# A gated mix of two attentions on one core: 776 instead of 756 score tiles on VectorE, in a new hand-laid order

## The chip, the cores and the metric

The kernel runs on one core of a Trainium2 chip. The metric is the device time of one execution in microseconds (us), the median of several runs. The engines of the core work side by side, each through its own list of instructions in order: TensorE (PE in the profile; PEld is its weight load), VectorE (DVE), ScalarE (ACT), GpSimd (POOL) and SyncE (SP, which only issues transfers here). They wait for one another through semaphores.

## The reference

The input x (2048 rows of 512, bf16) goes through two attentions with 32 heads of 16 each, and a gate mixes them. Part A is a linear attention with learnt softmax features, part B is ordinary softmax attention.

```
qkv = (x @ wqkv)                       # 32 heads of 16, for A and for B with weights of their own
# A
phi_q = [softmax(q @ w_phi), softmax(-q @ w_phi)];  phi_k likewise
o = phi_q @ (phi_k^T v) / (phi_q @ sum(phi_k) + 1e-6);   a = o @ A_wo
# B
p = softmax(q k^T / 4);   o = p v;     b = o @ B_wo
g = sigmoid(sum(x * gate_w))
out = g * a + (1 - g) * b
```

## The kernel before

Part B is nearly all of the work. It is cut into 32 blocks: a block is four heads and 512 queries. For each head of a block, the 2048 keys make 16 tiles of 128 keys by 512 queries, so a block has 64 score tiles and the kernel 2048. A score tile is one product (`qk_mm`, L994) that uses a strip of 32 rows of TensorE's array; the four heads of a block lie on four different strips, so up to four score products can run at once. Its result fills one bank of PSUM. There are six banks for scores (`bS`), one more for other work (`bM`) and one that gathers the weighted sums of a block (`bO`, `psO`).

A tile's exponential is made in one of two ways:

- On ScalarE: one instruction for two tiles in neighbouring banks (`add_exp`, L1115). The result goes to `Ebuf`, and one weighted sum for each tile (`pv_mm`, L1136) adds it to `psO`. Four such sums with 32 columns of the array each run at once.
- On VectorE: a conversion to int16 whose bits, read as bf16, are a rough exponential (`add_group`, L1084). Tiles go in groups of up to four. GpSimd adds a constant to all of a group's words in place of a second and a third conversion (`shifted`, L1060), and TensorE adds up all three versions in three weighted sums a tile (`add_pvd`, terms t, s and m). Two conversions of one group can be joined to one instruction over two banks (`Plan.join`, L1074); the table's `pairs` say which.

`DN` holds how many of each block's 64 tiles go to VectorE; its sum is 756. The groups of tiles use buffers in turn, from two rings (`PHASES`) that change at block 16 and at block 27.

Beside this run the projections of q, k and v for both parts, part A as a whole, the division by the sums of each block (a chain of small transfers through DRAM) and the output projection. Projections (`columns`, L754) use the array in strips of 32 columns, as the weighted sums do.

The order of each engine's instructions isn't found by the program when it is built: it is written out in `TABLE`, made beforehand by a planner that isn't in the file. Each number is the place of an operation in the list `P.ops`; an entry below zero stands for a filler, an operation that adds zeros or whose result nobody reads. `homes` gives the bank of each result. `Plan.place` reads the table, and `Plan.emit` writes the instructions with the waits that follow from data and banks. A wait is put in front of an instruction, and what stands behind it on its engine waits too.

At the start, `warm_fn` (L705) issues six products of ones while x is on its way.

Of the kernel before, what the change touches and what calls it, by code (L numbers as in the profile page):

```python
# [30 lines left out]
DN = (16, 24, 18, 24, 26, 26, 26, 20, 22, 22, 24, 18, 26, 24, 20, 26, 30, 22, 24, 26, 22, 24, 30, 26, 18, 22, 36, 18, 24, 24, 32, 16)  # L31
# [3 lines left out]
SIZES = (2, 2)  # L35
STICK = 58.273
# [59 lines left out]
    ),  # L96
    "act": (
# [32 lines left out]
    ),  # L130
# [465 lines left out]
def _build(ctx, nc, A_x, A_wqkv, A_w_phi, A_wo, B_wqkv, B_wo, gate_w, out):  # L596
# [105 lines left out]
    def warm_fn(e):  # L702
        ins = None
        for _ in range(6):
            ins = e.matmul(psM, lhsT=ones[:, 0:128], rhs=ones, start=True, stop=True)  # L705
        return ins
# [956 lines left out]
```

## Time and profile before

| | |
|---|---|
| median of 3 runs | 660.67 us |
| lowest and highest | 659.57 and 660.74 us |
| profiled execution, first to last instruction (span) | 657.6 us; the page has no other time of it |
| granted TensorE clock | 1.000 |
| PE busy | 649.1 us, 99% of the span |
| ACT busy | 635.1 us, 97% |
| DVE busy | 609.4 us, 93% |
| POOL busy | 410.8 us, 62% |

A busy engine in this table is one with at least one instruction under way; instructions overlap, matmuls above all, so the share doesn't say how densely they follow one another. For that the starts of instructions are read from the timeline. The chain of work that ended last is followed back from the last instruction, at each step to what released it or to the instruction before it on its engine. "x4" in a row of the timeline stands for four merged instructions.

### The profile page before, as it was taken

The page shows a single profiled execution, that of the slowest core. Times are in us where ns is not written, and L with a number is a line of the kernel's source. Part 1 is how long each engine was busy: PE and PEld are TensorE (multiplying, and loading weights), DVE is VectorE, ACT ScalarE, POOL GpSimd, SP SyncE. Part 2 cuts the span into 40 slices and gives each one's busy share as a digit, 9 for nine tenths or more (in the row PEclk, how much of TensorE's full clock was granted, in tenths as well). Part 3 has the DMA queues.
Part 4 walks back from the last instruction along what each step waited for, and adds up shares of the span by engine and source line. Part 5 has one row for each costly group of instructions (what it writes and reads, how often), then busy time and mean ns, then how long its engine had stood idle before and what let it go on. Part 6 is the DMA issues. An engine that isn't in the chain of part 4 may idle for free.

```text
span 657.6 us, 20651 instructions
## 1 busy us (share of the span) xinstructions
PE 649.1 (99%) x8820; PEld 227.3 (35%) x8820; DVE 609.4 (93%) x963; ACT 635.1 (97%) x720; POOL 410.8 (62%) x437
## 2 busy tenths in 40 slices
PE   8999999999999999999999999999999999999997
PEld 4333333434333333333233233322333333332333
DVE  6999899999998789999999999999999989999985
ACT  6999999999999999999999999999989999999996
POOL 7575367465665446486467876575867566656853
PEclk9999999999999999999999999999999999999999
DMA  6530101001010000000012431233211633134132
GB/s 131 104 100 12 33 12 27 11 11 19 11 27 10 16 18 8 19 17 14 23 37 47 100 77 33 63 78 68 48 51 35 102 56 83 35 63 103 44 84 48
DMA packets 67947, 30.94 MB, mean 47 GB/s; under 512 B 53208, under 2 KB 62808, under 8 KB 67856
## 3 DMA queue, kind: packets, MB, share of 16 engines
q1 hardware_dynamic: 65840, 28.82, 19.6%
q8 instruction: 69, 1.13, 0.7%
q10 hardware_dynamic: 1632, 0.79, 0.5%
q14 instruction: 22, 0.18, 0.1%
q0 software_dynamic: 384, 0.02, 0.1%
HBM read 7.87 MB, written 8.88 MB: 25 GB/s over the span
## 4 chain that ended last, share of the span: by engine, by line
PE 85%; DVE 12%; ACT 1%; issue 1%; DMA 1%; SPq 0%; DVEq 0%
PE psO L1136 32%; PE psS L994 30%; PE psS L754 15%; DVE Tx_t L1084 3%; PE psS L1417 3%; DVE Ty_t L1084 1%; DVE oT_t L1084 1%; DVE Wp_t L1084 1%; PE psS L842 1%; ACT E_t L1115 1%; DVE Tz_t L1084 1%; PE psS L1514 1%; PE psS L855 1%; PE psO L1126 1%; DMA phiK_t<-in_A_x_dram 1%
## 5 line engine op out<-in xcount | busy, mean ns | idle before, releaser
L1115 ACT ACTIVATE E_t<-psS 128x1024 bf16<-128x1024 f32 x643 | 601.9, 1068 | 11.2 <-PE psS L994 10.3
L994 PE MATMUL psS<-qz_t,kTB_t 32*128 32x512 bf16 (+1 forms) x2054 | 267.5, 383 | 2.8 <-ACT E_t L1104 0.6
L1084 DVE TENSOR_SCALAR Tx_t<-psS 128x512 int16<-128x512 f32 x246 | 163.2, 682 | 10.5 <-PE psS L994 9.4
L994 PEld LDWEIGHTS psS<-qz_t,kTB_t 32*128 32x128 bf16 x2054 | 71.8, 91 | 226.4 <-ACT E_t L1115 102.9
L1136 PE MATMUL psO<-E_t,vaug_t 128*32 128x512 bf16 x1292 | 119.0, 384 | 0.0
L1060 POOL INT64_ADD vA_t<-vA_t x72 | 71.6, 999 | 19.0 <-PE psO L1136 13.7
L1084 DVE TENSOR_SCALAR Ty_t<-psS 128x512 int16<-128x512 f32 x114 | 76.5, 682 | 4.8 <-PE psS L994 4.5
L1060 POOL INT64_ADD Ty_t<-Ty_t x42 | 44.0, 1048 | 18.5 <-PE psO L1136 18.1
L1060 POOL INT64_ADD Ty_t<-Tx_t x29 | 30.1, 1038 | 39.0 <-DVE Tx_t L1084 32.7
L1136 PE MATMUL psO<-vA_t,vaug_t 128*32 128x512 bf16 (+1 forms) x520 | 52.6, 384 | 0.0
L1136 PE MATMUL psO<-Ty_t,vaug_t 128*32 128x512 bf16 x440 | 45.4, 384 | 0.0
L1136 PEld LDWEIGHTS psO<-E_t,vaug_t 128*32 128x32 bf16 x1292 | 30.2, 95 | 39.5 <-issue 28.4
L1084 DVE TENSOR_SCALAR oT_t<-psS 128x512 int16<-128x512 f32 x62 | 41.7, 682 | 1.5 <-PE psS L994 1.0
L1084 DVE TENSOR_SCALAR Tz_t<-psS 128x512 int16<-128x512 f32 x60 | 40.2, 680 | 2.1 <-PE psS L994 1.8
L1060 POOL INT64_ADD vA_t<-Tx_t x22 | 22.7, 1032 | 31.0 <-DVE Tx_t L1084 24.1
L1060 POOL INT64_ADD phiQT_t<-Tx_t x19 | 18.9, 993 | 29.1 <-DVE Tx_t L1084 28.0
L1084 DVE TENSOR_SCALAR vA_t<-psS 128x512 int16<-128x512 f32 x54 | 36.2, 682 | 0.7 <-PE psS L994 0.3
L1084 DVE TENSOR_SCALAR WAT_t<-psS 128x512 int16<-128x512 f32 x52 | 35.2, 682 | 1.4 <-PE psS L994 1.2
L754 PE MATMUL psS<-Wp_t,xT_t 128*32 128x512 bf16 x512 | 35.8, 382 | 0.0
L754 PE MATMUL psS<-xT_t,WB_t 128*32 128x512 bf16 x480 | 34.9, 382 | 0.2
L1084 DVE TENSOR_SCALAR Wp_t<-psS 128x512 int16<-128x512 f32 x50 | 33.8, 683 | 0.9 <-PE psS L994 0.7
L1060 POOL INT64_ADD WoB_t<-oT_t x19 | 19.3, 1016 | 20.7 <-DVE oT_t L1084 16.5
(165 smaller groups left out, 920.1 us busy)
## 6 DMA issues: line engine op xcount, KB each, us to landing
dpq<-EA_t SPq DMA_DIRECT2D x16, 256.0 KB, 2.3
Rb_t<-lr SPq DMA_DIRECT2D x120, 32.0 KB, 1.9
dpo<-kv_t SPq DMA_DIRECT2D x16, 128.0 KB, 1.8
qz_t<-qz_t SPq DMA_DIRECT2D x120, 16.0 KB, 1.8
Tf_t<-Tf_t SPq DMA_DIRECT2D x60, 32.0 KB, 2.0
WB_t<-in_B_wqkv_dram SPq DMA_DIRECT2D x3, 384.0 KB, 3.6
out_dram<-WvA_t SPq DMA_DIRECT2D x8, 128.0 KB, 2.0
out_dram<-WB_t SPq DMA_DIRECT2D x6, 128.0 KB, 2.0
```

The costliest lines, as they stand in the source:

```text
L754: ins = e.matmul(out[32 * i:32 * i + 32, :], lhsT=lhsT[:, 32 * i:32 * i + 32], rhs=rhs, start=start, stop=stop, tile_position=(0, 32 * i))
L842: mms = [lambda e, ap, i=i, t=t: e.matmul(ap[:, 128 * i:128 * (i + 1)], lhsT=xT[:, t, NQ * c + 128 * i:NQ * c + 128 * (i + 1)], rhs=W_B[:, ...
L855: mms = [lambda e, ap, i=i, t=t: e.matmul(ap[:, 256 * i:256 * (i + 1)], lhsT=xT[:, t, NQ * c + 128 * (2 * hf + i):NQ * c + 128 * (2 * hf + ...
L994: return e.matmul(bank, lhsT=kT_B[32 * i:32 * i + 32, ROW[b // 2] % 2, 128 * kt:128 * (kt + 1)], rhs=qz[32 * i:32 * i + 32, b // 2 % 4, b ...
L1060: op = P.add("pool", P64 + W64 * size, d_prio(g["ts"][0]) - 5.0 + (0.0 if key == "s" else M_LATE), lambda e: e.int64_add(words(dst), words ...
L1084: ops.append(drain(f, mm, "dve", 0.70, d_prio(d), lambda e, ap, q=q: e.tensor_scalar(quarter(tb, q).bitcast(I16), ap, EXPB, 0.0, op0=ALU.a ...
L1115: op = P.add("act", EXP_OVH + 0.4267 * n, 0.0, lambda e: e.activation(Ebuf[:, j // 2 % EPAIRS, 512 * SZ[0] * (j % 2):512 * SZ[0] * (j % 2) ...
L1126: ins = e.matmul((psO if bank is None else bank)[32 * i:32 * i + 32, :], lhsT=zero[:], rhs=xT[:, 0, 0:NQ], start=bank is not None, stop=ba ...
L1136: return e.matmul(psO[32 * i:32 * i + w, :], lhsT=vaug[:, kt, o:o + w], rhs=rhs, start=start, stop=stop, tile_position=(0, 32 * i), skip_g ...
L1417: mms = [lambda e, ap, n=n, f=f: e.matmul(ap[:, 64 * n:64 * n + 64].rearrange("p (s g j) -> p s g j", s=2, j=4), lhsT=ident[:], rhs=es[n][ ...
L1514: mms = [lambda e, ap, g=g: e.matmul(ap[:, 64 * g:64 * g + 64], lhsT=qT(g)[:, 128 * j:128 * (j + 1)], rhs=kzbd[:, g, 0:64], start=True, st ...
```

## The change

Twenty tiles move from ScalarE to VectorE: ten entries of `DN` rise by 2. `TABLE` is new throughout: the order on all five engines, the banks, and the pairs of conversions. By the words that came with the change, the new order was laid out with GpSimd's and VectorE's use of a shared port on a first-come basis and with TensorE's signals spread out in time. What can be counted in the two tables:

| entries | before | after |
|---|---|---|
| SP | 259 | 259 |
| ACT | 693 | 683 |
| PE | 3017 | 3014 |
| of these fillers (below zero) | 23 | 1 |
| DVE | 963 | 1013 |
| POOL | 433 | 441 |
| pairs of conversions | 59 | 29 |

The warming products go from six to eight, a new kind of filler (-4, one product of ones into a score bank, with no wait for data) stands once near the start, and the two rings of buffers go on, at a change of phase, where the phase before stopped, in place of starting at their first buffer.

```
-DN = (16, 24, 18, 24, 26, 26, 26, 20, 22, 22, 24, 18, 26, 24, 20, 26, 30, 22, 24, 26, 22, 24, 30, 26, 18, 22, 36, 18, 24, 24, 32, 16)
+DN = (16, 24, 18, 26, 26, 26, 28, 20, 22, 24, 24, 18, 28, 24, 20, 26, 32, 22, 26, 26, 22, 26, 30, 26, 20, 22, 36, 20, 24, 24, 34, 16)
+TURNS = (0, 0)
 TABLE = {
     "pe": (
-        33, 72, 74, 86, 76, 80, 78, 88, 801, 803, 83, 807, 802, 804, 808, 90, 92, 93, 94, 95, 914, 912, 871, 867, 97, 98, 99, 100, 811,
...
+        33, 72, 74, -4, 86, 76, 80, 78, 88, 801, 803, 83, 807, 802, 804, 808, 90, 92, 93, 865, 914, 912, 817, 94, 95, 97, 98, 99,
...
         op = Op("pe", 0.215, 0.0, None, "idle")
-        op.deps, op.kind = list(self.ground), "zero"
+        op.deps, op.kind = [] if kind == -4 else list(self.ground), "zero"
...
-            op.fn = self.idle if kind == -1 else self.idle_o
+            op.fn = {-1: self.idle, -2: self.idle_o, -4: self.early}[kind]
...
     def warm_fn(e):
         ins = None
-        for _ in range(6):
+        for _ in range(8):
             ins = e.matmul(psM, lhsT=ones[:, 0:128], rhs=ones, start=True, stop=True)
...
-    count = [0] * len(PHASES)
+    count, at = [0] * len(PHASES), [(0, 0)]
     for n, g in enumerate(groups):
...
+        if g["ph"] == len(at):
+            more = count[g["ph"] - 1] - TURNS[g["ph"] - 1]
+            at.append(tuple((a + more) % len(ring) for a, ring in zip(at[-1], PHASES[g["ph"] - 1][1:])))
         count[g["ph"]] += 1
-        g["t"], g["s"] = rt[k % len(rt)], rs[k % len(rs)]
+        g["t"], g["s"] = (ring[(k + a) % len(ring)] for a, ring in zip(at[g["ph"]], (rt, rs)))
...
+    P.early = lambda e: e.matmul(psS[:, 1536:2048], lhsT=ones[:, 0:128], rhs=ones, start=True, stop=True)
```

More of the change, by code (lines that the diff above doesn't have):

```diff
@@ L349 @@
     "homes": (
-        "6705645027467514305342074350243502534104260164320524035135602350263510365015430143620420342604261461024510346013546026140264052310"
-        "5230152035062546025460520625306235102241052450613506452062540264506250426450624045260452452064052065420624502645032650624065235602"
-        "4506420523602520452360542654062405624062405624602560245560425605426504256024606254062554026504620562452406524056204254605240520462"
-        "0642506452602540562054260546256032065426042650420563206245065420253065426043260235602460250423015601350263506230654205230562450624"
@@ L354 @@
-        "6025602506452064250463260244502640241012654062504562406520462563020546202640526045265406250264540265604256034260352405246052064526"
-        "0462506426054260524560423106420602456054205462405620542654065240526404256045260542604256062504265405264062540625046256042605246504"
-        "2605642052402456053260524054205246054256024625064256105362053642045246502405642602305626504260532605320542504260452605426054620456"
-        "2045206425650465204653206523506420542606542064362036520630523230654206425602540654206254602654062540523052643034625042564052604534"
@@ L358 @@
-        "2035013640163561430163015042506245062406452604256042506452605260526025405240652045624562045604250646254065204526045620563263560365"
-        "0240564250436524062405240562405624062365024056254056204562406420546254062305623053620362036042650426503625032560245602460542502465"
-        "0326054625062450635206426402245403601360234502456035461052145042654062504260545216450620452640526045625406240652640524064250325602"
-        "4650320654206530624302456042505246052460264056240526045264026540260542650426052460254602546052460256045256042052540526506230564206"
@@ L362 @@
-        "524054025043560"
+        "6705645027467051435041234560351603610350625460532506245062054625062506452506325062460524056250642650246502450652406246504250426502"
+        "5406524025604562046264052064524605260452405620530416445036205632502356024560526045240652640530164024032651032146020142601420614621"
+        "4062140621042654025402543024532351036154205345234152054306240362463025360235106340153103416340613562035620352503210524150230513402"
+        "5124052034520325046520426540261046210420154201540251402514204502146026140264162041620416214325303165063251032501325031650351603561"
@@ new lines @@
+        "3561035163513051024501356431253026053605236052460524603015402156012402504526506210461053610531603563105630160315036156360153026350"
+        "2630526350362056320526350624506235024506246043260532603426054320643206430264032453205624056245604205623056425406240235012514036250"
+        "3240632460135025362035206320654205452016210642016402346240562540265402605462506352046206230524503265042532504530623506235026405624"
+        "0523650635023601364016431040364023462064230642310513605130154125102315032053215012305236502305630156302464063221352063620532062450"
@@ new lines @@
+        "6324603402463013051420353025360456250321503201524105214051240520354203452043540345051345102350123154205102450123150425140254301531"
+        "4613046120461260421540214501240521046203420125305420513205425140215021504126502450325063015361035015301653061305163420634620452026"
+        "4026402635206320663521041265042640126061351605310531630416240126504235032463104530164016240216046215413465130522062465042560320463"
+        "0135023460235602435130402346203431052316536013560264310530610351604301643026305235023506234602536203520653605320563256042506426023"
@@ L363 @@
+        "6103106310520604246404013"
     ),
@@ L416, in __init__ @@
         self.writer, self.readers = {}, {}
-        self.idle, self.idle_o, self.misc, self.every, self.never, self.ground = None, None, [], [], None, []
+        self.idle, self.idle_o, self.misc, self.every, self.never, self.ground, self.early = None, None, [], [], None, [], None
     def add(self, eng, dur, prio, fn, reads=(), writes=(), after=(), name="", sem=None, lat=0.0):
```

512 rows, old and new, of the table TABLE are left out of this document.

## The prediction

> **What bounds the kernel now.** I read four views in this order: the busy times and the chain of the page, the stretches of 60 us, the timeline of TensorE, and the waits. First the page: share of the span, instructions, and by engine the chain of work that ended last.
>
> ```profile
> span 657.6 us, 20651 instructions
> ...
> PE 649.1 (99%) x8820; PEld 227.3 (35%) x8820; DVE 609.4 (93%) x963; ACT 635.1 (97%) x720; POOL 410.8 (62%) x437
> ...
> PE 85%; DVE 12%; ACT 1%; issue 1%; DMA 1%; SPq 0%; DVEq 0%
> ```
>
> Three engines are nearly full, and the chain runs 85% through TensorE (PE). "Busy" alone doesn't say that an engine works at its pace, so I look at the paces. The timeline gives starts and durations (us); I read starts against starts.
>
> ```profile
> 200.95 0.60 PE L994 MATMUL psS<-qz_t,kTB_t 32*128 32x512 bf16 x5
> ...
> 642.29 0.40 PE L1136 MATMUL psO<-E_t,vaug_t 128*32 128x512 bf16 x4
> 642.52 0.39 PE L1136 MATMUL psO<-vA_t,vaug_t 128*32 128x512 bf16 x4
> 642.84 0.39 PE L994 MATMUL psS<-qz_t,kTB_t 32*128 32x512 bf16 x3
> 643.16 0.40 PE L1136 MATMUL psO<-E_t,vaug_t 128*32 128x512 bf16 x4
> 643.38 0.39 PE L1136 MATMUL psO<-vA_t,vaug_t 128*32 128x512 bf16 x4
> ```
>
> Four weighted sums (L1136, one for each strip of 32 columns) start together and the next four start 0.22 us later (643.16 to 643.38): this is one PE step. From sums to score products (L994, strips of 32 rows) it takes 0.32 (642.52 to 642.84) and back again 0.32 (642.84 to 643.16). So each alternation between the two costs 0.10 above a step. Three score products on different strips take 0.39 in all, but the five at 200.95 take 0.60: a product whose strip is taken by an earlier one of the same run adds 0.21, one more step.
>
> The paces of the other two engines, from rows that merge several instructions of one kind, and from the chain:
>
> ```profile
> 203.74 2.87 ACT L1115 ACTIVATE E_t<-psS 128x1024 bf16<-128x1024 f32 x3
> 641.22 1.89 DVE L1084 TENSOR_SCALAR Ty_t<-psS 128x512 int16<-128x512 f32 x3
> 50.10 1.13 DVE Tz_t L1074
> ```
>
> With the mean durations of the groups below (1068 and 682 ns), an exponential of two tiles follows another after (2.87 - 1.07) / 2 = 0.90 us on ScalarE (ACT), and a conversion of one tile on VectorE (DVE) after (1.89 - 0.68) / 2 = 0.60. A paired conversion (two tiles, L1074) holds the chain for 1.13.
>
> ```profile
> L1115 ACT ACTIVATE E_t<-psS 128x1024 bf16<-128x1024 f32 x643 | 601.9, 1068 | 11.2 <-PE psS L994 10.3
> L1084 DVE TENSOR_SCALAR Tx_t<-psS 128x512 int16<-128x512 f32 x246 | 163.2, 682 | 10.5 <-PE psS L994 9.4
> L1060 POOL INT64_ADD vA_t<-vA_t x72 | 71.6, 999 | 19.0 <-PE psO L1136 13.7
> L1247 DVE TENSOR_TENSOR oT_t<-Tf_t,Rb_t 128x512 bf16<-128x512 f32 x15 | 10.7, 716 | 0.0
> ```
>
> Now the stretches (us busy and instructions of PE, weight loads, DVE, ACT, POOL; then granted clock, DMA share, GB/s):
>
> ```profile
> 60.00:120.00 60.00, 60.00 (x855) 20.95 (x843) 54.52 (x85) 60.00 (x72) 33.35 (x36) 1.00 0.11 21
> 180.00:240.00 60.00, 59.97 (x857) 20.57 (x854) 51.94 (x79) 59.94 (x72) 31.79 (x36) 1.00 0.08 18
> 300.00:360.00 60.00, 59.00 (x806) 19.88 (x798) 57.83 (x98) 59.19 (x68) 37.99 (x38) 1.00 0.11 27
> 360.00:420.00 60.00, 59.88 (x794) 19.81 (x790) 58.61 (x89) 60.00 (x69) 43.89 (x44) 1.00 0.32 73
> ```
>
> In 60:120, 180:240 and 360:420 ACT has no idle time to speak of: there it is a bound of its own beside PE. DVE is fullest in 360:420 (58.61 of 60) and has 8 us to spare in 180:240. At one place DVE alone carries the chain without a break; a few of its pieces:
>
> ```profile
> 306.14 1.20 DVE Tz_t L1084 x2
> 307.34 0.60 DVE Tx_t L1084
> 307.94 0.60 DVE vaug_t L862
> ```
>
> The waits, last (us in total, times, longest):
>
> ```profile
> PEld psS L994 <- ACT E_t L1115: 102.9, 258, 0.6
> PEld psO L1136 <- issue: 87.0, 360, 0.4
> ...
> ACT E_t L1115 <- PE psS L994: 10.3, 27, 0.8
> DVE Tx_t L1084 <- PE psS L994: 9.4, 25, 1.1
> ```
>
> The 102.9 look like a stall of PE behind ACT, but 102.9 / 258 is 0.40 each, and an alternation puts 0.32 between two starts whether anybody is waited for or not, so most of it is the alternation itself. PE works near its pace, ACT is just behind, and DVE is third.
>
> **The change part by part.** The counts of operations below are counted in DN and in the order tables, those of the kernel and those of the diff; none is a time.
>
> *Twenty tiles from ACT to DVE.* ACT does 646 exponentials before ((2048 - 756) / 2: 643 in the row above and three done in halves) and 636 after: 10 x 0.90 = 9.0 us less. This counts where ACT is a bound, the three full stretches, 180 of 657.6 us: -2.5. Where PE ends last it is worth nothing.
>
> *DVE.* The pairs in the table fall from 59 to 29, so single conversions go from 638 to 718: 80 x 0.60 - 30 x 1.13 = 48.0 - 33.9 = +14.1 us. DVE idles 657.6 - 609.4 = 48.2 us, which hides it on the whole; it isn't hidden where DVE carries the chain. The longest such place, around 300 us, is fed by blocks 13 to 15 (block 13 begins at exponential 270 of 646), and their DN isn't raised. I take +0.4, for the pairs that are split there. Bounds: 0, and 12% of the time at 14.1 / 609.4, that is +1.8. If the cover is gone, see the first rival.
>
> *PE, more sums.* The groups go from 198 to 202, each with three terms; the sums over exponentials go from 337 operations to 334, one step each. 12 - 3 = 9 steps more, at 0.22: +2.0 us.
>
> *PE, fillers.* 23 filler operations of four zero products leave (the table has 23 entries of -1, and none after). 23 x 0.22 = 5.1 us. The row of the source view and its busy tenths over 40 slices:
>
> ```profile
> L1126 PE MATMUL psO<-xT_t,zero_t x92: 379/379/390, 17.2 to 595.9; 128*32 128x512 bf16 x92
> ...
> busy tenths in 40 slices 0110000000010000000000223430002000012000
> ```
>
> Most stand in slices 23 to 27 (360 to 440 us), where ACT and DVE are full and PE would have waited; so the bounds are 0 and -5.1 and I take half, -2.5.
>
> *PE, order of the score products.* In the old order 107 score products find their strip of rows taken in their run, in the new one 81: 26 x 0.21 = -5.5. Runs of score products go from 595 to 600, and all changes between row-wise, column-wise and whole-array work from 1222 to 1227: +5 x 0.10 = +0.5. Bounds of the first: 0, where the second product waited for its bank anyhow, and -5.5. I take -5.5, by the x5 row, where nothing but the strip held it.
>
> PE together: +2.0 - 2.5 - 5.5 + 0.5 = -5.5 us, between +2.5 and -8.1. It counts where PE sets the end, outside the stretches given to ACT (27%) and DVE's 12%: 61% of it, -3.4.
>
> *The start.* Two more warming products, and one more (entry -4) behind the first two transposes of x. Here is the start, and the load that the chain waits for:
>
> ```profile
> 0.77 2.72 PE L705 MATMUL psS<-const-bfloat16-1.0 128*128 128x512 bf16 x6 [0.77 <-PEq L1648]
> 3.33 0.58 PE L1529 MATMUL psS<-ident_t,phiK_t 128*128 128x128 bf16 x4
> ...
> 5.91 0.40 PE L1529 MATMUL psS<-ident_t,phiK_t 128*128 128x128 bf16 x4 [0.35 <-DMA phiK_t<-in_A_x_dram]
> ...
> 1.65 4.21 DMA phiK_t<-in_A_x_dram
> ```
>
> The six take 2.72, about 0.43 apart, so two more push the first transpose from 3.33 to about 4.2 and the products behind it by as much, less what they waited for loads. The transposes at 5.91 wait for the load that ends at 5.86 whatever comes before, so I cost it at 0; without that cover it is +0.9, and a clock that comes up earlier could give back a few tenths (four 128-column products took 0.58 at 3.33 and 0.40 at 5.91).
>
> *POOL and SP.* Groups of four go from 180 to 186 and groups of two from 18 to 16. Each has two shifted adds; a whole one takes 1.0 us, so POOL gains 12 adds of 1.0 and loses 4 shorter ones: about +10 on 410.8. It stays off the path unless an add comes late for its sums; behind it on POOL are only further adds. SP issues 259 operations before and after, in another order; of the chain 1% is DMA, so I take 0. The ring of buffers now goes on where the phase before it stopped: no instruction changes.
>
> *First-come port use.* That POOL's adds and some DVE operations hold each other up shows in one row: the 15 products of L1247 average 716 ns against 682 of the conversions, 15 x 0.03 = 0.5 us, all off PE. So a layout that avoids it can bring at most about that, and I put down 0. The Trainium skill's page "SBUF — State Buffer" ("Who interferes with whom") says that a DVE instruction with two SBUF inputs and a GpSimd instruction that reads SBUF exclude each other, the loser waiting the whole instruction through. By that rule the 15 could wait up to 1.0 us each, an estimate of 15 us on DVE to be saved. The trace agrees on the direction and not on the size; were it so, the time would fall as in the third rival, whose chance holds it.
>
> **Sum:** -2.5 (ACT) - 3.4 (PE) + 0.4 (DVE) = -5.5, so a span of 652.1. The page gives no time of the profiled execution beside its span; the median of the runs shown, 660.67, is 3.07 above it. 652.1 + 3.1 = 655.2, and I say 655.
>
> **The rivals.**
>
> *DVE becomes the bound (slower).* It has one fixed order, and each conversion frees a bank that a score product waits for. In 360:420 it has 1.4 us of 60 left, and +14.1 over the kernel is 1.3 for each 60. It decides if DVE keeps the waits it has now: then it needs 609.4 + 14.1 + 48.2 = 671.7 of span, 674.8 in time; with half of the waits kept, 650.7. The break-even is at 34 us of the 48.2. For it: thirty pairings are given up at the same time as the load rises. Against it: 8 us are free in 180:240, and DVE's waits in the groups above are for PE, which the change relieves. I say 667, between 663 and 675.
>
> *Nothing comes of it.* The strips that were taken twice waited for banks anyhow, the fillers stood in waits, and ACT isn't on the chain (1%): PE is then +2.5, less what ACT's full stretches give, -2.5. Time 660.7, between 658 and 663. For it speaks that chain; against it that PE's waits for ACT are mostly alternations, so PE's steps do count.
>
> *More than the counts say.* PE's steps shrink by the whole 8.1 and the waits of ACT for PE (10.3 of the 11.2) go too, ACT then takes its 9.0 over the whole kernel: 657.6 - 9.0 = 648.6 of span, 651.7, and down to 645 if part of those 10.3 goes.
>
> *The clock falls without the fillers (slower).* The granted clock is 1.00 in all stretches quoted. If a gap grew long enough to lose it, steps would take about twice as long for a while, as at the start (0.58 against 0.40): six such losses of 3 us each, with the steps in them at half pace, cost about 9 us: 664 on top of the forecast, 670 on top of no gain. Against it: the longest wait of PE in the rows above is 0.6 us, and a filler adds only 0.22 to one. The Trainium skill's page "TensorE: Matmul & The Clock Gate" ("HAM oscillation") says that a PE left idle for more than about 3.4 us goes back to half its clock; no run here shows that, and no gap here is near it.
>
> **How the numbers follow.** As summed: 0.52, with its own range of 651 to 659. More: 0.14. Nothing: 0.17. DVE: 0.14. Clock: 0.03. The range that leaves out about 2 in 10 runs from 647 to 663. About 0.2% (1.3 us) is what a measurement of this kernel can tell from no change. Faster by more: 0.52 + 0.14 + 0.04 of "nothing" = 0.70; within: 0.10; slower: 0.03 + 0.14 + 0.03 = 0.20.
>
> **What would show it.** Right: about 633 exponentials in the row of L1115, the same pace of 0.90, no L1126 in the middle, ACT busy near 626, PE's share of the chain at 80% or more, and runs of score products with fewer long rows. Wrong: DVE's share of the chain at 25% or more, with long rows of waits of PE's weight loads for Tx_t and Ty_t; or a granted clock under 1.00; or ACT's idle time before L1115 (11.2) above 20, which would mean that the saved exponentials came back as waits.

## The result, and the profile after

The changed kernel takes 654.65 us (median of 4 runs, 654.29 to 655.40), the kernel before 660.12 us on the same chip (4 runs, 658.95 to 660.74). The ratio is 0.9913 with a 95% interval of 0.9889 to 0.9938: 5.5 us faster, against a forecast of 655.0. A second set of runs gave 0.9918 [0.9905, 0.9932]. The profiled execution took 655.01 us with a span of 653.1, so the time lies 1.9 us above the span.

The page after: span, busy time, share of the span and instructions of an engine, and by engine the chain of work that ended last.

```profile
span 653.1 us, 20595 instructions
...
PE 646.6 (99%) x8771; PEld 229.7 (35%) x8771; DVE 615.8 (94%) x1013; ACT 626.6 (96%) x710; POOL 420.4 (64%) x445
...
PE 85%; ACT 10%; DVE 4%; issue 0%; DVEq 0%
```

The loads moved as counted: ACT from 635.1 to 626.6 us busy, DVE from 609.4 to 615.8, POOL from 410.8 to 420.4. The chain changed its second engine. DVE had 12% of it and ACT 1%; now ACT has 10% and DVE 4%. DVE has more work and yet less of the chain, so this comes with the new order (the split pairs are part of it) and not from the load.

The groups after (busy, mean ns of one, idle time before and its releaser; L1131 are the exponentials, L1100 the conversions, L1076 POOL's adds):

```profile
L1131 ACT ACTIVATE E_t<-psS 128x1024 bf16<-128x1024 f32 x633 | 592.4, 1059 | 15.3 <-PE psS L1010 14.5
...
L1100 DVE TENSOR_SCALAR Tx_t<-psS 128x512 int16<-128x512 f32 x268 | 175.3, 680 | 3.5 <-PE psS L1010 2.7
...
L1076 POOL INT64_ADD vA_t<-vA_t x68 | 68.6, 1014 | 19.4 <-PE psO L1152 19.0
```

There are ten exponentials fewer (633 for 643). ACT's idle time before them rose from 11.2 to 15.3 us, so part of the saved work came back as waits. DVE's idle time before Tx_t fell from 10.5 to 3.5. Now the stretches of 60 us, in the columns used before:

```profile
60.00:120.00 60.00, 60.00 (x845) 21.79 (x846) 55.63 (x92) 59.29 (x71) 35.55 (x39) 1.00 0.09 21
...
180.00:240.00 60.00, 59.94 (x855) 21.34 (x851) 54.53 (x86) 59.27 (x70) 35.88 (x39) 1.00 0.09 18
...
300.00:360.00 60.00, 59.94 (x841) 20.86 (x842) 59.38 (x100) 59.26 (x68) 39.04 (x40) 1.00 0.16 45
360.00:420.00 60.00, 59.95 (x810) 20.64 (x802) 59.24 (x99) 59.50 (x71) 45.26 (x46) 1.00 0.31 76
```

In 60:120, 180:240 and 360:420 ACT was at 60.00, 59.94 and 60.00 busy; it now has a little air. DVE is fuller in all four, 59.4 of 60 around 300 us, where it carried the chain before. There the chain after reads (start, duration, engine, product):

```profile
304.20 0.55 PE psO L1152 x8
304.75 0.34 PE psS L1010 x4
305.08 0.54 PE psO L1152 x8
```

That is TensorE alternating between sums and scores at its own pace: 0.55 for eight sums is two steps and one change (0.22 + 0.32). DVE is fuller here and nobody on the chain waits for it.

I read the same gain from three ledgers, each made from all starts of one engine in the two traces: its work at pace (the time between two starts when nothing holds the second), and its idle time above pace.

| from first to last instruction of the kind | work at pace | waits above pace |
|---|---|---|
| PE, all products | 620.7 to 616.7 (-4.0) | 32.4 to 32.0 (-0.4) |
| ACT | 620.8 to 611.7 (-9.1) | 30.7 to 35.2 (+4.5) |
| DVE | 595.4 to 609.1 (+13.7) | 58.6 to 41.2 (-17.4) |

By this ledger PE turned its 4.0 us into time almost in full, ACT gave half of its 9.1 back as waits, and DVE took on 13.7 and lost 17.4 of waits. How PE's row splits depends on the paces: with one fixed pace for a step (0.21 to 0.22) and one for an alternation (0.32) the same starts give -2.9 and -1.5. Its sum, -4.4, doesn't depend on them; DVE's row is good to about 1 us.

By kinds of product on PE, each run of one kind timed to the start of the next: scores -3.5, sums +3.0, fillers -7.1, projections +4.4 (cut off by scores more often: 127 times for 103), products over the whole array -1.2.

Where these 4.4 us lie shows when both traces are cut at the same score products, counted by their starts:

| score products | before | after |
|---|---|---|
| 1000th to 1400th | 122.7 us, with 56 filler and 232 projection products | 122.2 us, with 0 and 304 |
| 1400th to 1800th | 124.5 us, with 8 and 368 | 119.7 us, with 0 and 272 |

The first stretch (323 to 446 us before) is the one in which most fillers stood. It takes the same time in both orders, but the new one has 72 projection products there in place of the fillers. The stretch behind it has 96 fewer (their time falls by 6.0 us), and is 4.8 us shorter. So the new order does useful work where the old one only filled. That moving these projections alone would bring the gain isn't shown: no run does that.

### The profile page after: what moved, and what is told of

Its sections match the earlier page's. It is cut to its first block, busy times and chain, and to the rows that moved or that the text cites. A ratio compares the mean times of both kernels' runs of the same rounds, so it can differ in the third digit from the quotient of the medians.

```text
span 653.1 us, 20595 instructions
## 1 busy us (share of the span) xinstructions
PE 646.6 (99%) x8771; PEld 229.7 (35%) x8771; DVE 615.8 (94%) x1013; ACT 626.6 (96%) x710; POOL 420.4 (64%) x445
## 4 chain that ended last, share of the span: by engine, by line
PE 85%; ACT 10%; DVE 4%; issue 0%; DVEq 0%
PE psO L1152 32%; PE psS L1010 30%; PE psS L767 15%; ACT E_t L1131 10%; PE psS L1433 2%; PE psS L868 1%; PE psS L855 1%; DVE Tx_t L1100 1%; PE psS L1530 1%; DVE Ty_t L1100 1%; PE psS L1517 1%; PE psS L718 1%; DVE vA_t L1100 1%; DVE Wp_t L1100 0%; PE psS L1392 0%; PE psS L1473 0%
## 5 line engine op out<-in xcount | busy, mean ns | idle before, releaser
L1131 ACT ACTIVATE E_t<-psS 128x1024 bf16<-128x1024 f32 x633 | 592.4, 1059 | 15.3 <-PE psS L1010 14.5
L1100 DVE TENSOR_SCALAR Tx_t<-psS 128x512 int16<-128x512 f32 x268 | 175.3, 680 | 3.5 <-PE psS L1010 2.7
L1010 PEld LDWEIGHTS psS<-qz_t,kTB_t 32*128 32x128 bf16 x2054 | 72.9, 91 | 224.2 <-ACT E_t L1131 112.5
L1152 PE MATMUL psO<-E_t,vaug_t 128*32 128x512 bf16 x1272 | 124.4, 385 | 0.0
L1100 DVE TENSOR_SCALAR Ty_t<-psS 128x512 int16<-128x512 f32 x122 | 81.2, 683 | 5.5 <-PE psS L1010 5.2
L1076 POOL INT64_ADD vA_t<-vA_t x68 | 68.6, 1014 | 19.4 <-PE psO L1152 19.0
L1152 PE MATMUL psO<-vA_t,vaug_t 128*32 128x512 bf16 x534 | 53.1, 385 | 0.0
L1100 DVE TENSOR_SCALAR Tz_t<-psS 128x512 int16<-128x512 f32 x74 | 49.0, 681 | 2.5 <-PE psS L1010 2.0
L1076 POOL INT64_ADD Ty_t<-Ty_t x43 | 43.3, 1008 | 10.1 <-PE psO L1152 9.0
L1152 PEld LDWEIGHTS psO<-E_t,vaug_t 128*32 128x32 bf16 x1272 | 32.4, 95 | 42.8 <-issue 33.5
L1100 DVE TENSOR_SCALAR oT_t<-psS 128x512 int16<-128x512 f32 x66 | 43.9, 682 | 3.2 <-PE psS L1010 2.4
L1152 PE MATMUL psO<-Ty_t,vaug_t 128*32 128x512 bf16 (+1 forms) x450 | 45.9, 385 | 0.0
L1100 DVE TENSOR_SCALAR vA_t<-psS 128x512 int16<-128x512 f32 x66 | 44.1, 681 | 0.9 <-PE psS L1010 0.7
L1100 DVE TENSOR_SCALAR WAT_t<-psS 128x512 int16<-128x512 f32 x66 | 43.8, 680 | 0.4 <-PE psS L1010 0.4
L767 PE MATMUL psS<-Wp_t,xT_t 128*32 128x512 bf16 x512 | 41.2, 382 | 0.0
L1100 DVE TENSOR_SCALAR Wp_t<-psS 128x512 int16<-128x512 f32 x56 | 37.5, 681 | 0.5 <-PE psS L1010 0.5
L1076 POOL INT64_ADD phiQT_t<-Tx_t x19 | 19.3, 1015 | 22.9 <-DVE Tx_t L1100 20.7
L1076 POOL INT64_ADD Ty_t<-Tx_t x24 | 23.6, 984 | 15.6 <-DVE Tx_t L1100 15.5
L1076 POOL INT64_ADD WoB_t<-oT_t x19 | 18.9, 993 | 20.5 <-DVE oT_t L1100 18.5
L1076 POOL INT64_ADD WoA_t<-Tz_t x19 | 19.7, 1039 | 15.7 <-DVE Tz_t L1100 7.8
```

The source lines that it names most:

```text
L767: ins = e.matmul(out[32 * i:32 * i + 32, :], lhsT=lhsT[:, 32 * i:32 * i + 32], rhs=rhs, start=start, stop=stop, tile_position=(0, 32 * i))
L1010: return e.matmul(bank, lhsT=kT_B[32 * i:32 * i + 32, ROW[b // 2] % 2, 128 * kt:128 * (kt + 1)], rhs=qz[32 * i:32 * i + 32, b // 2 % 4, b ...
L1076: op = P.add("pool", P64 + W64 * size, d_prio(g["ts"][0]) - 5.0 + (0.0 if key == "s" else M_LATE), lambda e: e.int64_add(words(dst), words ...
L1100: ops.append(drain(f, mm, "dve", 0.70, d_prio(d), lambda e, ap, q=q: e.tensor_scalar(quarter(tb, q).bitcast(I16), ap, EXPB, 0.0, op0=ALU.a ...
L1131: op = P.add("act", EXP_OVH + 0.4267 * n, 0.0, lambda e: e.activation(Ebuf[:, j // 2 % EPAIRS, 512 * SZ[0] * (j % 2):512 * SZ[0] * (j % 2) ...
L1152: return e.matmul(psO[32 * i:32 * i + w, :], lhsT=vaug[:, kt, o:o + w], rhs=rhs, start=start, stop=stop, tile_position=(0, 32 * i), skip_g ...
```

## The experiments

My theory was the sum of the prediction: fillers, taken strips and ACT's load each bring their part, and DVE's additions hide. The rivals: PE ends last everywhere, so that each step saved on PE counts in full and a relief of ACT brings nothing (A); the fillers keep the clock up (B); a taken strip stands in a wait, so that untangling it brings nothing (C); ACT is the bound (D); only the new order as a whole gains (E); DVE has become the bound (F). All ratios are against the kernel before on the same chip.

**One relief at a time, on the old order.** Three edits of the kernel before: without the 23 fillers; with 15 pairs of tiles swapped within their groups, so that 17 score products fewer find their strip taken; and with 21 exponentials over one tile in place of two, 21 x (1054 - 638 ns) = 8.7 us less for ACT by the means in its trace.

```
old_nofill:  + TABLE["pe"] = tuple(k for k in TABLE["pe"] if k != -1)
old_strips:  + SWAPS = ((856, 858), (865, 869), ...)     # 15 pairs of score products
             + for a, k in SWAPS: swap a with k in TABLE["pe"], a + 1 with k + 1 in TABLE["dve"]
old_half:    + HALF = tuple(range(12, 642, 30))
             + w = n - (j in HALF)                       # tiles that exponential j covers
```

> The old order without its 23 fillers (four zero products each), all else as before. Mine, from the sum of the prediction: they stood in waits for the most part, so half of 5.1 us at most: 0 to -2.5, I expect -1.5 us against the kernel before (ratio 0.998). Rival A (PE ends last everywhere, so each of its steps counts): the 7.1 us that the fillers and the gaps behind them take in the old trace come off whole, ratio 0.989 to 0.992. Rival B (the fillers keep the clock up): granted clock under 1.00 and a longer time.

> The old order with 15 swaps of two tiles within their group, so that 17 fewer score products find their strip of rows taken in their run; nothing else moves. Mine: each is worth one step on PE (322 ns for a run without, 534 with one), 17 x 0.21 = 3.6 us of PE's work; the part that reaches the end as in the prediction's sum, 0.61 of it: -2.2 us, ratio 0.9967. Rival A (PE ends last everywhere): -3.6, 0.9945. Rival C (a taken strip stands in a wait for a bank): 0, 1.000.

> The old order, with 21 of the 646 exponentials, spread over the kernel, done for their first tile only (the second tile's result is left out, its bank is freed with the first): ScalarE has 21 x 0.43 = 9.0 us less to do, as after the change, and nothing else differs. Mine: only where ACT is a bound beside PE, 27% of the span: -2.5 us, ratio 0.996. Rival D (ACT is the bound): -9, 0.986. Rival A (PE ends last everywhere): 0.

Measured: 1.0003 [0.9990, 1.0016] without fillers, 1.0002 [0.9988, 1.0015] with the swaps, 1.0001 [0.9991, 1.0011] with the lighter ACT. The bounds leave at most 0.7, 0.8 and 0.6 us of gain (0.10%, 0.12% and 0.09% of 660); by my sum's weights they were worth 1.5 (2.5 at 61%), 2.2 (17 x 0.21 = 3.6 at 61%) and 2.4 (8.7 at 27%). In the traces, the swaps took 0.5 us off the time of the score products on PE, not 3.6, so the rest must have come back as waits there. Without the fillers, the stretch from the 1000th to the 1400th score product still takes 122.2 us (122.7 with them). ACT's busy time fell by 5.3 us (635.1 to 629.8), and it waits longer: its exponentials waited 10.3 us in 27 waits before, and in old_half (total, times, longest):

```profile
ACT E_t L1117 <- PE psS L995: 14.5, 41, 0.9
```

My theory fell here. Rival C holds, within 0.8 us. Rival A is right for ACT alone: it asked for 7.1 us from the fillers and 3.6 from the swaps, and neither came. B's lower clock didn't show either (1.000 without fillers).

**All three together on the old order**, and the changed kernel itself beside it.

```
old_all:  the three edits above in one kernel
new_again: the changed kernel, unedited
```

> The three together on the old order: no fillers, 17 fewer taken strips, 21 exponentials for one tile only (the second tile's result is left out). Mine: PE and ACT are bounds in turn, so a relief of both brings more than the sum of the parts: -1.5 - 2.2 - 2.5 = -6.2 at least, -8 if so; ratio 0.988 to 0.991, that is the gain of the change or more without its new order. Rival E (the new order itself, its fewer waits, is what gains): -3 at most, 0.995 or above.

> The changed kernel itself again, beside the three that follow, so that they can be compared with it on one chip. Every theory: ratio to the kernel before 0.991 as measured.

Measured: 0.9991 [0.9979, 1.0002], 659.01 us; the changed kernel 0.9918 [0.9905, 0.9932], 654.56. So with fewer steps on PE and nearly the same relief for ACT, and without a microsecond more on DVE, the old order gains at most 1.4 us, as rival E has it. From old_all's page:

```profile
PE 646.7 (98%) x8728; PEld 227.1 (35%) x8728; DVE 608.3 (93%) x963; ACT 628.7 (96%) x720; POOL 411.0 (63%) x437
...
PE 81%; DVE 15%; ACT 1%; issue 1%; DMA 1%; POOL 0%; SPq 0%
```

PE is busy for as long as after the change (646.7 and 646.6) and the kernel isn't faster. PE's work at pace is 615.0, 5.7 less than before; its waits are 37.5, 5.1 more. DVE's share of the chain rose from 12% to 15%, and I asked next whether DVE holds it.

**The same with a lighter DVE.** 34 single conversions cover 64 of 512 columns.

```
old_light: old_all, and   w = 64 if q == 0 and g["n"] % 5 == 2 and g["n"] > 9 else NQ
```

> The old order relieved on all three engines: no fillers, 17 fewer taken strips and 21 exponentials for one tile only, as in old_all, and 34 single conversions narrowed from 512 to 64 columns (the rest of those tiles is left out), 34 x 0.47 = 16 us less on VectorE. old_all, without the last, gained 0.6 us although PE and ACT had 6 to 9 us less to do. Theory G (the three engines are bounds in turn, and in old_all DVE was the one left): 5 to 7 us faster than old_all, ratio 0.989 to 0.992. Theory H (what is left is the fixed order: each engine waits where the order makes it wait for the hand-over of another, whatever its load): under 2 us against old_all, 0.996 to 0.999.

Measured: 0.9977 [0.9965, 0.9989], 658.71 us (before: 659.55). Its page:

```profile
PE 646.5 (98%) x8728; PEld 226.4 (34%) x8728; DVE 595.7 (91%) x963; ACT 629.0 (96%) x720; POOL 410.7 (63%) x437
...
PE 84%; DVE 8%; ACT 6%; DMA 1%; issue 1%; POOL 0%; SPq 0%
```

DVE has 12.6 us less to do, and its share of the chain fell to 8%, but the time fell by 0.1% to 0.35% of the kernel before. PE's waits stand at 38.1. Theory G falls, and H's forecast holds: reliefs of 6 to 13 us on all three engines leave the old order at 659. That the hand-overs between the engines hold it there is what remains, not something that a run singles out, and which of them stays open.

**More strips untangled on the new order**: ten more swaps, 12 fewer taken strips (83 to 71; the prediction's 81 leaves out the first, narrower products).

> The changed kernel with 10 swaps of two tiles within their group, so that 12 fewer score products find their strip taken. Mine: 12 x 0.21 = 2.5 us of PE's work, 0.61 of it at the end: -1.5 us against the changed kernel. Rival A (PE ends last everywhere): -2.5. Rival C (a taken strip stands in a wait): 0.

Measured: 0.9916 [0.9902, 0.9929], 654.40 us, next to 654.56 unedited. Nothing, on this order either. No kernel that computes everything came out ahead of the changed one.

**Additions on the new order.** On DVE, 16 reciprocals of a tile nobody reads, spread over its list; on ACT, 19 copies of such a tile.

```
new_dve:  + 16 x P.add("dve", ..., lambda e: e.reciprocal(spare[:], spare[:]), ...)      # 128x128 f32
new_act:  + 19 x P.add("act", ..., lambda e: e.activation(spare[:], spare[:], ACTF.Copy), ...)  # 128x512 bf16
          + row.insert(int(size * (0.05 + 0.90 * n / 16)) + n, ...)                      # 19 for ACT
```

> The changed kernel with 16 more instructions on VectorE, spread evenly (a reciprocal of 128 x 128 values in place in a tile that nobody else uses, 0.87 us each as in the rows of L1432): +14 us of DVE work, as much again as the change brought. Mine: DVE still has 37 us of idle time and hides nearly all: +1 to +2 us against the changed kernel. Rival F (DVE has become the bound): +7 or more.

> The changed kernel with 19 more instructions on ScalarE, spread evenly (a copy of 128 x 512 values in place in a tile that nobody else uses, 0.5 to 0.6 us each): +9 to +11 us of ACT work, as much as the change took away. Mine: +2.5 to +4 us against the changed kernel. Rival D (ACT is the bound): +9 to +11. Rival A (PE alone ends last): 0 to +1.

Measured: DVE 1.0093 [1.0079, 1.0107], 666.23 us, 11.7 above the unedited kernel; ACT 1.0056 [1.0043, 1.0069], 663.44 us, 8.9 above. Their pages, DVE's first:

```profile
PE 652.2 (98%) x8771; PEld 228.9 (34%) x8771; DVE 628.2 (94%) x1029; ACT 630.0 (95%) x710; POOL 420.8 (63%) x446
...
PE 72%; DVE 20%; ACT 6%; issue 1%; SPq 0%; DMA 0%; DVEq 0%
```

```profile
PE 651.0 (98%) x8771; PEld 229.5 (35%) x8771; DVE 618.5 (93%) x1013; ACT 636.0 (96%) x729; POOL 421.0 (64%) x446
...
PE 62%; ACT 35%; DVE 2%; issue 0%; DVEq 0%
```

The reciprocals last 0.94 us each, 15.1 together, and the copies 12.7 together, but they overlap with their neighbours: DVE's busy time is 12.5 us longer than in the unedited kernel's run of this set, ACT's 9.1, and nearly all of either is in the time. DVE's additions go into the time although it still idles for 37 us of 665.1. POOL's busy time moved by 0.4 us, so the reciprocals didn't slow the adds. F's price came true, and D's nearly (8.9 for 9 to 11), though both engines can't be the one bound. My reading, which no run singles out: what is added between two hand-overs makes the next one late, and idle time elsewhere doesn't help.

**PE nearly alone.** In both kernels, nearly all exponentials over one tile and all conversions from group 44 on (about 155 us) on 64 columns. Now ACT and DVE have air, and PE's own order should set the time.

```
old_pe, new_pe:  + HALF = tuple(range(12, 630));   w = n - (j in HALF)
                 + w = 64 if g["n"] >= 44 else NQ          # singles and pairs
```

> The old order and all its products, with ScalarE and VectorE nearly free: all exponentials but those of the first 12 and last 16 slots for one tile only, and all conversions from group 44 on narrowed to 64 columns (the rest is left out). What is left is PE with its own order. Theory G and H: PE's waits for banks go, its 620.7 us at pace stay, with a start of 8 and a tail of 4: 630 to 642 us. If ACT were the bound all along it would be under 620; if PE had no part of its idle time from the others, no change (660).

> The same with the changed kernel. By PE's work at pace (616.7 us against 620.7) it is 4 us faster than old_pe. If it is as far ahead as the kernels are of each other (5.3), the gain of the change is PE's own; if it isn't ahead, the gain comes from how the engines meet.

Measured: on the old order 0.9845 [0.9824, 0.9867], 649.96 us; on the new one 0.9731 [0.9709, 0.9752], 642.23 us. The first lies 8 us above the upper end of what I expected, and the gap of 7.7 us is larger than the 4 to 5.3 that I expected. Their pages, the old order first:

```profile
PE 641.5 (99%) x8820; PEld 219.2 (34%) x8820; DVE 369.0 (57%) x963; ACT 426.3 (66%) x720; POOL 409.7 (63%) x437
...
PE 92%; DVE 6%; POOL 1%; DMA 1%; issue 0%; SPq 0%; ACT 0%
```

```profile
PE 634.2 (99%) x8771; PEld 218.8 (34%) x8771; DVE 373.4 (58%) x1013; ACT 419.1 (65%) x710; POOL 419.4 (66%) x445
...
PE 93%; SPq 4%; POOL 1%; DMA 0%; DVE 0%; issue 0%; DVEq 0%
```

With a third of ACT's and 40% of DVE's work gone, 98% of the time is still there: PE's list, with the waits that are left in it, takes 650 of 660 us in the old order and 642 of 655 in the new. By the criterion set for new_pe, the gain of the change is PE's own. At pace PE's work differs by 5.9 (615.4 and 609.5), its waits by 2.5; about 29 and 26 us of waits remain, since the other engines are lighter and not free. A part of the gap may be DVE's, which in the first 155 us has its whole load in both kernels and has 6% of the chain in the old order, nothing in the new. At the 500th score product (167.4 and 164.8 us) the new order is 2.6 us ahead, 0.9 of it before the first one.

**Six warming products in the changed kernel**, and no early product into a score bank:

```
new_warm:  -for _ in range(8):   +for _ in range(6):
           + TABLE["pe"] = tuple(k for k in TABLE["pe"] if k != -4)
```

> The changed kernel with six warming products as before and without the one product of entry -4. In the profiles so far the first product of q was done at 1.2 GHz pace in three of five runs of the old order and the first exponential came at 8.7 us there, at 7.4 to 8.0 in the others and in all five of the new. Mine: the two products and the early one are worth 0.5 us in the mean, so +0.5 us against the changed kernel (ratio to before 0.9925), with the first exponential at 7.6 or at 8.7 us. Rival (the extra products only delay the start, as the profile of the change suggests): -0.3 us.

Measured: 0.9925 [0.9903, 0.9946], 654.89 us. The first exponential starts at 7.67 us. In the time, six products can't be told from eight (0.9918 for the unedited kernel, in another set).

## Why the prediction was right, and where its steps were not

- **Time, direction and loads held.** 655.0 against 654.65. 633 exponentials, ACT busy 626.6 ("near 626"), no fillers of L1126, PE 85% of the chain, DVE 4% where 25% would have refuted it, the granted clock 1.00 in the stretches, ACT's idle time 15.3 where over 20 would have refuted it.
- **The sum was right for a wrong reason.** The step that failed is the weighting: "ACT counts in its full stretches (27%), PE in 61%". By it ACT's 9.0 alone were worth 2.5 us, but old_half (8.7) shows 0 to 0.6 on the old order; fillers and strips alone bring 0 to 0.8 each, and all three together 0 to 1.4. The share of the time in which an engine is full isn't the share of a saving that is kept. The likely reason is that with a fixed order on five engines a saved step ends at the next hand-over, which comes when it came before. The sum had no term for the new order, such as the projections that now stand where the fillers stood. That its 5.5 us came out to the tenth is luck.
- **PE's steps: near on the whole, by misses that offset.** I counted -5.5, between +2.5 and -8.1; the two traces show -4.4, and PE nearly alone -7.7, some of it perhaps DVE's. A taken strip costs what I took: runs of score products without one take 322 ns (median of 495 before, 323 ns of 527 after), with one taken twice 535 to 538 (95 and 67), 0.21 us more. In the kernels themselves scores fell by 3.5 us on PE, not by 5.5; with PE nearly alone, where fewer waits hide it, they fell by 5.7. The fillers took 7.1 us of PE's time with them, where I counted half of 5.1. The projections, to which I gave nothing, rose by 4.4 (4.2 with PE nearly alone). One such strip after the change, in the timeline of TensorE:

```profile
201.33 0.60 PE L1010 MATMUL psS<-qz_t,kTB_t 32*128 32x512 bf16 x4
...
202.62 0.39 PE L1010 MATMUL psS<-qz_t,kTB_t 32*128 32x512 bf16 x3
202.94 0.40 PE L1152 MATMUL psO<-oT_t,vaug_t 128*32 128x512 bf16 x4
```

  Four products take 0.60 when two share a strip, three on different strips 0.39. From scores to sums it is again 0.32 against a step of 0.22. The Trainium skill's page "TensorEngine Tiling (Array Packing)" ("Key Properties") says that a change of tiling mode drains TensorE; the trace agrees, with 0.10 us for each.
- **PE's waits for ACT** were read rightly as alternations. The waits of weight loads after (total, times, longest):

```profile
PEld psS L1010 <- ACT E_t L1131: 112.5, 288, 0.6
PEld psO L1152 <- issue: 87.2, 373, 0.4
...
ACT E_t L1131 <- PE psS L1010: 14.5, 34, 0.8
```

  They grew from 102.9 to 112.5 us while the kernel got faster; 112.5 / 288 is 0.39 each, hardly more than a change takes anyhow.
- **"DVE's idle time hides 14 us" fell as a rule.** The 14 were no loss in the new order: DVE's idle time above pace fell from 58.6 to 41.2 with them. But 12.5 us put evenly into DVE's list of the new kernel cost 11.7, nearly what the rival "DVE becomes the bound" charged for its 14.1. That rival had the right price for a DVE load nobody had planned for, and the wrong case.
- **"Nothing comes of it"** is right for each part on the old order and wrong for the change.
- **What the change is worth where:** by ratios, the lighter ACT and DVE of PE nearly alone are worth 1.55% on the old order (1 - 0.9845, 10 us) and 1.87% on the new one (0.9918 - 0.9731, 12 us). PE nearly alone got 7.7 us shorter and 5.3 of that arrive. How much is due to the tile counts and how much to the order stays open: no run has the old counts in a new order.
- **The start, costed at 0:** the first exponential starts at 8.01 us, 7.63 before. From the start of the first to that of the last one it was 636.8 us, 641.2 before. So -4.4 lie between them, +0.4 before the first and -0.5 behind the last, in this execution. The time between span and measured time, 3.07 in my sum, was 1.9; I had set the median of three runs against the span of one, and execution by execution it is 1.9 before as well (659.46 us with a span of 657.6). The span came out at 653.1, 1.0 above my 652.1, and the two misses cancel.

## What to carry to other kernels

In this kernel, whose order is fixed on all engines, reliefs of 4 to 9 us on one of them were worth 0.8 us at most until the order was laid out anew, and additions of 9 and 12 us of busy time cost nearly their full length; so neither busy shares nor idle time price an edit there. Measure instead how much shorter one engine's list became: make the other engines' work much lighter in both versions and time them. Look also at what the new order puts where the old one waited. Count a packed TensorE's list in steps, with a price for each change of mode and each strip taken twice.

## What the runs showed of the hardware

- **The clock at the start, and a granted clock that doesn't show it.** With eight warming products (3.57 us) and the early one the four first q products took 0.60 to 0.66 us in six profiles of six; with six (2.72 us) they took 1.06 in five of eight, little more than half the pace. Seven of these eight have the old order; the one with the new order, new_warm, took 0.60. Two profiles of the unedited changed kernel differ too, first the one shown above, then that of the second set (timeline of TensorE; L1644 is the early product, L841 and L881 the first projections):

```profile
4.99 0.64 PE L1644 MATMUL psS<-const-bfloat16-1.0 128*128 128x512 bf16 x1
5.41 0.63 PE L841 MATMUL psS<-xT_t,WB_t 128*128 128x128 bf16 x4
6.06 0.61 PE L1545 MATMUL psS<-ident_t,phiK_t 128*128 128x128 bf16 x4
6.46 0.66 PE L881 MATMUL psS<-xT_t,WB_t 128*128 128x256 bf16 x4
```

```profile
4.99 0.61 PE L1644 MATMUL psS<-const-bfloat16-1.0 128*128 128x512 bf16 x1
5.41 0.41 PE L841 MATMUL psS<-xT_t,WB_t 128*128 128x128 bf16 x4
6.16 0.40 PE L1545 MATMUL psS<-ident_t,phiK_t 128*128 128x128 bf16 x4 [0.34 <-DMA phiK_t<-in_A_x_dram]
6.39 0.60 PE L881 MATMUL psS<-xT_t,WB_t 128*128 128x256 bf16 x4
```

  In the first the clock comes up at about 6.5 us, in the second at about 5.4. In old_all, with six, it hasn't yet come up for the q products:

```profile
6.07 0.61 PE L1532 MATMUL psS<-ident_t,phiK_t 128*128 128x128 bf16 x4 [0.61 <-DMA phiK_t<-in_A_x_dram]
6.47 1.06 PE L870 MATMUL psS<-xT_t,WB_t 128*128 128x256 bf16 x4
```

  The granted clock is 1.00 in the first 20 us throughout, so the paces have to be read, not that column. The first exponential then starts at 8.5 to 8.8 us in place of 7.4 to 8.0: about 1 us, below what the times of so long a kernel tell. The Trainium skill's page "TensorE: Matmul & The Clock Gate" ("Part 1: The HAM clock gate") says that the clock rises after a window of some 3.4 us that runs on its own, so that the same kernel differs from run to run; the two profiles above agree, and what sets the moment isn't shown here.
- **Removing on the old order and adding on the new one came out unlike.** 5.3 us of ACT's busy time off: 0 to 0.6 gained (old order). 9.1 on: 8.9 lost (new order). I had expected 2.5 to 4 for the second. No run adds to the old order or relieves ACT by as little on the new one, so whether the direction or the order makes the difference isn't shown.
- **A DVE product with both inputs in SBUF waits for POOL's add to end.** The prediction spread the 716 ns of L1247 over its 15 products and laid the difference to the shared port. In the trace fourteen of them take 675 to 686 ns and one takes 1200: it starts while an add of POOL has 0.66 us left, and ends 0.54 us behind that add's end. The same shows in all fourteen profiles, for the two kinds of DVE product with both inputs in SBUF (L1247 and L1444): each of the 46 that took over 720 ns started during an add and ended 0.54 to 0.55 us behind its end. The kernels lose little by it, one such product before (1200 ns) and two after (801 and 735). Where the narrowed conversions shifted DVE's work, in old_pe and new_pe, there are 11 and 13, up to 1408 ns.
